# Three transfers of weight words moved to another queue, and ten products moved in front of a join

## The chip, the cores and the metric

The kernel runs on one core of a Trainium2 chip. The metric is the time of one execution on the device, in microseconds (us). Six names occur throughout: TensorE (PE in the profile) multiplies matrices, VectorE (DVE) and ScalarE (ACT) work elementwise, GpSimd (POOL) does the rest, SyncE (SP) only issues transfers, and the DMA engines carry them. ScalarE and GpSimd issue transfers as well, in the order of their own instructions.

## The reference

Two blocks follow one another: a DeltaNet recurrence over 768 tokens for 4 x 8 heads of 48, and a feed-forward block on its output with a layer norm in front and a residual.

```python
# attention: q, k, v of (4, 8, 768, 48), beta of (4, 8, 768)
k_n = k / (np.linalg.norm(k, axis=-1, keepdims=True) + 1e-06)
for t in range(S):
    kt, vt, bt = k_n[:, :, t], v[:, :, t], beta[:, :, t, None]
    y[:, :, t] = np.einsum('bhd,bhde->bhe', q[:, :, t], state)
    v_old = np.einsum('bhde,bhd->bhe', state, kt)
    state = state + bt[:, :, :, None] * np.einsum('bhd,bhe->bhde', kt, vt - v_old)
# bridge: (B, H, S, D) -> x of (4, 768, 384); w_ch1 of 384 x 1536, w_ch2 of 1536 x 384
xn = (x - mu) / np.sqrt(var + 1e-06) * g_ln
out = x + np.maximum(xn @ w_ch1, 0.0) @ w_ch2
```

The weights arrive as 64-bit floats. The kernel gets them as pairs of 32-bit words and makes 32-bit floats of them itself.

## The kernel before

The 768 tokens are cut into twelve chunks of 64. Within a chunk the recurrence becomes a triangular system: the products of the keys (gram, `gsb`) are inverted block by block (VectorE eliminates row after row, names `xb`, `tmp`), and a join puts the inverted blocks of 32 rows together into `xt` with small matmuls (`p_e`, `p_z`). The recurrence of the chunk then needs `xt` (`p_u`), the state (`p_k`, `p_y`, `p_s`), and hands its output, normalised, to the feed-forward block. That block is one chunk behind, so its large products fill TensorE while the recurrence waits.

The weights come in twelve pieces of 768 KB of words, with three buffers for them. A piece is fetched into a buffer and converted in five steps, one on ScalarE and four on VectorE; the next fetch waits until its buffer is free.

```python
    def fetch_words(eng=nc.gpsimd, held=False):
        if len(words) < len(pieces):
            src = pieces[len(words)][1]
            words.append(early_pool.tile([128, WN, 2], U32, name="words", bufs=3))
            if held:
                nc.vector.memset(words[-1][0:1, 0:1, 0].bitcast(FP32), 0.0)
            ...
            eng.dma_start(out=out_, in_=src)
```

With `held`, the first fetch has to wait for a memset of one element, and so for VectorE's place in its program. The start of the kernel, in the order that every engine keeps (`next` runs a generator to its next yield):

```python
        inv = first_blocks(two)                  # blocks of 16 rows of chunks 0 and 1
        for _ in range(3):
            next(inv)                            # gather, roots of the diagonal (ScalarE), scaling
        load_blocks(q, 0, 1, (nc.scalar,))       # eight transfers on ScalarE's queue
        load_kv(0, nc.scalar)                    # four of k, two of v (v_raw), on the same
        for gen in grams_01:
            next(gen, None)                      # ScalarE: four copies of p_g to gsb, line 372
        ...
        for i in range(FB // 2):
            next(inv)                            # VectorE: two rows of the elimination each
            if i == 4:
                for n in range(3):
                    fetch_words(nc.sync, held=(n == 0))
                keep_warm(3, mark=True)          # matmuls on zeros, to keep the clock up
        knrm = norm_parts(0, xts[NXT - 1])
        next(knrm)                               # ScalarE: squares of k, lines 404 and 406
        parts = [to_fp32(i) for i in range(3)]
        joining = first_join(0)
        next(joining)                            # x_n, p_e (line 598), es (ScalarE, line 601)
        turned(0, 1)                             # q turned, VectorE
        knrm = next(knrm)                        # sums (VectorE) and root (ScalarE)
        for piece in parts[0:2]:
            next(piece)                          # first conversion step of words, ScalarE, line 302
        for _ in range(3):
            next(parts[0])                       # lines 304, 306, 310, VectorE
        next(joining)                            # p_z (line 606), own + p_z (line 607)
        ...
        nc.vector.memset(tblocks[3][0:1, 0, 0, 0:1], 0.0)   # line 891: marker for the loads behind it
        load_blocks(q, 1, 1, (nc.sync,))
        load_kv(1)
```

From chunk 2 on a chunk has a slot, written as a list of names in the order of issue; each engine takes its own part of it in that order. The names that matter here: `H` is one product p_h of the hidden layer (six instructions on TensorE) with its relu on ScalarE; `KQ`, `U`, `S`, `PU` are the recurrence's products p_k and p_y, p_u, p_s, and p_y; `P1` to `P7` are the seven half-size products of the second layer (p_a, p_o), `S1` to `S4` and `d1` to `d7` the sums before and after them on VectorE; `R` is all that is left of the rows of an elimination and `r` two rows; `own`, `xt` and `xn` turn and hand over the inverted blocks, `J` is one step of the join, and an apostrophe says that it belongs to the pair of chunks in hand and not to the next; `ga`, `sq`, `no` begin the next pair's inversion (a zeroing on ScalarE and a turning on VectorE; a root on ScalarE; scaling on VectorE). `TQ` and `PT` turn q and multiply it with k, `L1` and `L2` are the layer norm.

The join's three steps on a pair of chunks:

```python
    def join(chunks, both=False):
        ...
        yield                                    # xn: two turnings on VectorE
        for c, xn in zip(chunks, xns):           # J, J
            for h in range(GH):
                for e in range(2):
                    nc.tensor.matmul(p_e[r1, h], gsb[r0, h, BK:C], xn[r0, h])
                if last:
                    last_z(*last, h)             # p_z of the first chunk between the p_e of the second
            if last:
                end_z(*last)                     # half the copy to xt on VectorE, half on ScalarE
            ...                                  # es on ScalarE
            yield
        for h in range(GH):                      # J
            last_z(*last, h)
        end_z(*last)
        yield
```

Of the kernel before, what the change touches and what calls it, by code (L numbers as in the profile page):

```python
# [8 lines left out]
FP32 = mybir.dt.float32  # L9
# [40 lines left out]
@contextmanager  # L50
def in_this_order(tc):

    first = len(tc.nc.cur_bb.bb.instructions)
    last = {}
    yield last
    for ins in tc.nc.cur_bb.bb.instructions[first:]:
        if ins.engine not in ORDERED:
            continue
        if ins.engine in last:
            tc.add_manual_dep(  # L60
                ins, last[ins.engine].name,
                mybir.DependencyInfo(mybir.DependencyClass.NoSync, mybir.DependencyReason.DATA),
                reason="in_this_order",
            )
        last[ins.engine] = ins
# [17 lines left out]
def kernel(  # L83
# [22 lines left out]
    nc = tc.nc  # L106
    B, H, S, D = q.shape
# [41 lines left out]
    def load_blocks(src, c, n, engs):  # L149
        dst = tblocks[(2 * c + n) % NTB]  # L150
        for u in range(2):
            toks = slice(c * C + 32 * u, c * C + 32 * u + 32)
            for hp in range(2):
                for m in range(2):
                    w = min(32, D - 32 * m)
                    p0 = DP * hp + 32 * m
                    engs[m % len(engs)].dma_start(
                        out=dst[p0 : p0 + 32, :, u, 0:w],
                        in_=src[:, hp::2, toks, 32 * m : 32 * m + w].rearrange("b j t d -> t (b j) d"),
                    )  # L160

    def load(dst, src, c, eng):
        for e in range(2):
            eng.dma_start(
                out=dst[e * C : (e + 1) * C],
                in_=src[2 * e : 2 * e + 2, :, c * C : (c + 1) * C, :].rearrange("g h p d -> p (g h) d"),
            )

    def load_k(c, eng):

        for n in range(2):
            for e in range(2):
                eng.dma_start(
                    out=k_of(c)[(e ^ n) * C : (e ^ n) * C + C, n::2],
                    in_=k[2 * e : 2 * e + 2, n::2, c * C : (c + 1) * C, :].rearrange("g h p d -> p (g h) d"),
                )
# [4 lines left out]
    def load_kv(c, eng=nc.sync):  # L181
        load_k(c, eng)
        vs[c] = loads.tile([128, GH, D], FP32, name="v_raw")
        load(vs[c], v, c, eng)
# [23 lines left out]
    ]  # L208
    words = []

    def fetch_words(eng=nc.gpsimd, held=False):
        if len(words) < len(pieces):
            src = pieces[len(words)][1]
            words.append(early_pool.tile([128, WN, 2], U32, name="words", bufs=3))
            if held:
                nc.vector.memset(words[-1][0:1, 0:1, 0].bitcast(FP32), 0.0)
            out_ = words[-1].rearrange("p n w -> p (n w)")
            if len(src.shape) == 3:
                out_ = out_.rearrange("p (t n) -> p t n", t=2)
            eng.dma_start(out=out_, in_=src)  # L220
# [114 lines left out]
    def turned(c, n, more=False):  # L335

        made[c][n] = work.tile([128, GH, C], FP32, name="kq"[n] + "t", bufs=(4, 2)[n])
        nc.vector.transpose(
            made[c][n].rearrange("p i (u t) -> p i u t", t=32), tblocks[(2 * c + n) % NTB]
        )  # L340
        if more and c + 2 < NCH:
            load_blocks((k, q)[n], c + 2, n, (nc.sync,))
# [6 lines left out]
    def gram(c, fine=False, maker=ps_two):  # L349

        kt = made[c][0]
        p_g = ps_g(maker)
        for j in range(GP):
            for u in range(2) if fine else (0,):
                for hp, e in TILES:
                    rows = slice(DP * hp, DP * hp + D)
                    i = e * GP + j
                    r0 = BK * u
                    out_ = p_g[C * e + r0 : C * e + r0 + (BK if fine else C), hp, j, 0 : C - r0]
                    nc.tensor.matmul(  # L360
                        out_, kt[rows, i, r0 : r0 + (BK if fine else C)], kt[rows, i, r0:C]
                    )
        dst = grams[c].rearrange("p (j n) t -> p n j t", n=2)
        if fine:
            nc.scalar.copy(dst[:, :, :, 0:BK], p_g[:, :, :, 0:BK])
            yield
        else:
            nc.scalar.copy(dst, p_g)
        for e in range(2):
            if fine:  # L370
                rows = slice(C * e, C * e + BK)
                nc.scalar.copy(dst[rows, :, :, BK:C], p_g[rows, :, :, BK:C])
            else:
                rows = slice(C * e + BK, C * e + C)
                nc.scalar.copy(dst[rows, :, :, 0:BK], p_g[rows, :, :, BK:C])
# [49 lines left out]
    def new_chunk(c):  # L425
        if c % SLAB == 0:
            pairs[c // SLAB] = work.tile([128, SLAB, GH, C], FP32, name="gsb", bufs=2)
        grams[c] = pairs[c // SLAB][:, c % SLAB]
        made[c] = {}
# [391 lines left out]
    def begin(c):  # L821
        xs[c] = work.tile([128, 2, DM], FP32, name="x_ln")
        xnts[c] = work.tile([128, KC, TOK], FP32, name="xnt")

    def keep_warm(n, width=8, mark=False):

        if mark:
            nc.vector.memset(zeros[0:1, 0:1], 0.0)  # L828
        p_w = ps_ffn([128, 8, 64], "p_w")
        for _ in range(n):  # L830
            nc.tensor.matmul(  # L831
                p_w[0:64, 0:width], zeros, zeros[:, None, :].to_broadcast([128, width, 64]),
                start=True, stop=True,
            )

    two = range(2)
    with in_this_order(tc) as last:
        grams_01 = []
        keep_warm(3)
        for c in two:  # L840
            new_chunk(c)
            turned(c, 0)
            grams_01.append(gram(c, fine=True, maker=(ps_two, ps_by)[c]))
            next(grams_01[c])

        keep_warm(46, 1)
        inv = first_blocks(two)
        for _ in range(3):
            next(inv)
        load_blocks(q, 0, 1, (nc.scalar,))  # L850
        load_kv(0, nc.scalar)
        for gen in grams_01:
            next(gen, None)
        nc.vector.tensor_copy(out=scale_w[:, 0, 0:KC], in_=g_sb)
        nc.vector.tensor_scalar_mul(scale_w[:, 1, 0:KC], g_sb, 2.0**-52)
        for i in range(FB // 2):
            next(inv)
            if i == 4:
                for n in range(3):
                    fetch_words(nc.sync, held=(n == 0))  # L860
                keep_warm(3, mark=True)
        knrm = norm_parts(0, xts[NXT - 1])
        next(knrm)
        parts = [to_fp32(i) for i in range(3)]
        joining = first_join(0)
        next(joining)
        turned(0, 1)
        knrm = next(knrm)
        for piece in parts[0:2]:
            next(piece)  # L870
        for _ in range(3):
            next(parts[0])
        next(joining)
        masking = product(0)
        next(masking)
        to_xt(0)
        joining = join((0,), both=True)
        next(joining)
        next(parts[0], None)
        fetch_words()  # L880
        next(joining)
        next(parts[2])
        scale_v(0, knrm)
        keep_warm(1)
        for _ in joining:
            pass
        for _ in masking:
            pass
        keep_warm(1)

        nc.vector.memset(tblocks[3][0:1, 0, 0, 0:1], 0.0)
        load_blocks(q, 1, 1, (nc.sync,))
        load_kv(1)
        for c in (2, 3):
            load_blocks(k, c, 0, (nc.sync,))
        load_beta()
        begin(0)
        recur_0 = recur(0)
        next(recur_0)
        next(recur_0)  # L900
        keep_warm(1)
        for _ in range(3):
            next(parts[1])
        next(recur_0)
        next(parts[1], None)
        fetch_words()
        next(recur_0)
        keep_warm(4)
        next(recur_0)
        next(parts[2])  # L910
        next(recur_0)
        for _ in parts[2]:
            pass
        fetch_words()
# [42 lines left out]
    with behind(tc, after):  # L957
# [10 lines left out]
        3: """KQ H H sq H no H r H r U TQ(a2) H r H r H r S H r H r H H PU P1 L1 S1 S2 d1 PT(a2)  # L968
            P2 d2 L2 S4 P6 d6 S3 TK(a4) P5 d5 r N r P7 d7 G(a4) TK(b4) P3 d3 r G(b4) Vk P4 d4 r
            Vn Vs""",  # L970
        4: """KQ H H R' own' H H H xt' xn' ga H J' H H sq J' no U H J' r H r S H r TQ(b) H r PU P1
            L1 S1 S2 d1 PT(b) P2 d2 L2 S4 P6 d6 S3 r P5 d5 r N r P7 d7 r P3 d3 r Vk P4 d4 Vn Vs""",
        5: """KQ H r H r H r H r H R U TQ(a2) H H own TK(a4) H S H H xt H xn H PU P1 L1 S1 S2 d1
            PT(a2) P2 d2 L2 S4 P6 d6 S3 TK(b4) J P5 d5 G(a4) N P7 d7 J P3 d3 G(b4) J P4 d4
# [105 lines left out]
```

## Time and profile before

| | |
|---|---|
| time, median of 3 runs | 578.1 us (577.19, 578.1, 581.67) |
| span of the profiled run | 575.6 us |
| mean granted TensorE clock | 0.956 |
| TensorE busy | 533.7 us, 93% |
| VectorE busy | 394.6 us, 69% |
| ScalarE busy | 173.3 us, 30% |
| HBM read | 28.43 MB |

The page cuts the span into 40 slices of 14.4 us and gives the busy share of each in tenths; the row PEclk is the share of the full clock that was granted. A timeline lists the instructions of one engine by start and duration in us; the brackets at the end of a line hold the idle time just before, and what ended it. "ACTq" and "SPq" are issues of transfers from ScalarE and SyncE; their duration is that of the issue and not that of the transfer. Where a wait is for several things at once, the one that came last is named.

### The profile page before, as it was taken

The page shows a single profiled execution, that of the slowest core. Times are in us where ns is not written, and L with a number is a line of the kernel's source. Part 1 is how long each engine was busy: PE and PEld are TensorE (multiplying, and loading weights), DVE is VectorE, ACT ScalarE, POOL GpSimd, SP SyncE. Part 2 cuts the span into 40 slices and gives each one's busy share as a digit, 9 for nine tenths or more (in the row PEclk, how much of TensorE's full clock was granted, in tenths as well). Part 3 has the DMA queues.
Part 4 walks back from the last instruction along what each step waited for, and adds up shares of the span by engine and source line. Part 5 has one row for each costly group of instructions (what it writes and reads, how often), then busy time and mean ns, then how long its engine had stood idle before and what let it go on. Part 6 is the DMA issues. An engine that isn't in the chain of part 4 may idle for free.

```text
span 575.6 us, 20679 instructions
## 1 busy us (share of the span) xinstructions
PE 533.7 (93%) x9386; PEld 459.4 (80%) x9386; DVE 394.6 (69%) x816; ACT 173.3 (30%) x352; POOL 15.4 (3%) x36
## 2 busy tenths in 40 slices
PE   6769797889999996999999999999999999999996
PEld 3445576468898895798888898888898988988996
DVE  4856978999858789499964899736899540523212
ACT  1043352512253242422335322245213232222120
POOL 5000111000000000000000000000000000000000
PEclk9767999999699999899999999999999999999999
DMA  4545968871065144023432304203213010010101
GB/s 58 119 131 114 225 152 212 135 113 30 5 77 97 24 53 87 3 30 70 56 44 60 55 2 84 30 10 77 30 27 59 2 31 1 2 30 1 27 1 27
DMA packets 158390, 34.47 MB, mean 60 GB/s; under 512 B 153680, under 2 KB 156768, under 8 KB 158304
## 3 DMA queue, kind: packets, MB, share of 16 engines
q1 hardware_dynamic: 144208, 24.63, 25.1%
q0 software_dynamic: 1456, 7.10, 3.8%
q10 hardware_dynamic: 12640, 1.44, 1.9%
q8 instruction: 73, 1.20, 0.9%
q14 instruction: 13, 0.11, 0.1%
HBM read 28.43 MB, written 4.72 MB: 58 GB/s over the span
## 4 chain that ended last, share of the span: by engine, by line
PE 65%; DVE 15%; issue 12%; ACT 3%; DMA 3%; POOL 1%; POOLq 0%; DVEq 0%; ACTq 0%
PE p_h L732 26%; PE p_a L787 13%; PE p_o L787 9%; DVE tmp L545 4%; DVE xb L550 4%; PE p_g L360 2%; DMA words<-in_moe_w_ch_dram 2%; PE p_u L651 2%; PE p_y L671 2%; PE p_s L663 2%; PE p_z L614 2%; PE p_g L385 2%; PE p_k L640 1%; PE p_e L570 1%; PE p_y L640 1%
## 5 line engine op out<-in xcount | busy, mean ns | idle before, releaser
L732 PE MATMUL p_h<-xnt,w_sb 128*128 128x256 f32 x864 | 200.6, 389 | 4.3 <-ACT h L736 1.9
L732 PEld LDWEIGHTS p_h<-xnt,w_sb 128*128 128x128 f32 x864 | 163.4, 193 | 29.0 <-issue 2.7
L736 ACT ACTIVATE h<-p_h 128x256 f32<-128x256 f32 x144 | 55.1, 384 | 154.6 <-PE p_h L732 147.8
L550 DVE TENSOR_TENSOR xb<-xb,tmp 128x31 f32<-128x31 f32 (+20 forms) x170 | 56.9, 335 | 5.8
L545 DVE TENSOR_TENSOR tmp<-xb,gb 128x31 f32<-128x31 f32 (+15 forms) x155 | 52.5, 339 | 4.2
L787 PE MATMUL p_o<-w_sb,h 128*128 128x192 f32 x264 | 49.1, 337 | 0.0
L787 PE MATMUL p_a<-t,h 128*128 128x192 f32 x264 | 47.2, 329 | 0.5 <-DVE o L792 0.5
L787 PEld LDWEIGHTS p_o<-w_sb,h 128*128 128x128 f32 x264 | 43.8, 193 | 0.8
L787 PEld LDWEIGHTS p_a<-t,h 128*128 128x128 f32 x264 | 42.7, 190 | 1.2 <-DVE o L792 0.8
L682 DVE BATCH_NORM_STATS2 st<-x_ln 128x6 f32<-128x384 f32 x24 | 13.0, 544 | 36.3 <-ACT x_ln L676 36.2
L831 PE MATMUL p_w<-zeros 128*64 128x64 f32 (+1 forms) x118 | 26.1, 388 | 7.4 <-DVE zeros L828 4.2
L787 PE MATMUL p_a<-t,s 128*128 128x192 f32 x132 | 24.1, 333 | 0.4 <-DVE o L792 0.4
L787 PE MATMUL p_a<-w_sb,h 128*128 128x192 f32 x132 | 24.2, 333 | 0.0
L787 PE MATMUL p_o<-w_sb,s 128*128 128x192 f32 x132 | 23.6, 328 | 0.0
L699 ACT COPY xnt<-p_n 128x384 f32<-128x384 f32 x24 | 10.4, 483 | 43.3 <-PE p_n L698 43.2
L570 PEld LDWEIGHTS p_e<-x_n,gsb 32*32 32x32 f32 x768 | 15.4, 115 | 9.9 <-DVE x_n L561 6.9
L570 PE MATMUL p_e<-x_n,gsb 32*32 32x32 f32 x768 | 17.0, 202 | 6.6 <-DVE x_n L561 6.4
L581 ACT ACTIVATE es<-p_e 32x512 f32<-32x512 f32 x23 | 13.6, 589 | 31.6 <-PE p_e L570 31.3
L787 PEld LDWEIGHTS p_a<-t,s 128*128 128x128 f32 x132 | 22.2, 195 | 0.8 <-DVE o L792 0.7
L831 PEld LDWEIGHTS p_w<-zeros 128*64 128x64 f32 x118 | 10.8, 166 | 14.6 <-issue 6.7
L360 PEld LDWEIGHTS p_g<-kt 48*64 48x64 f32 (+1 forms) x896 | 13.3, 130 | 11.1 <-issue 4.8
L787 PEld LDWEIGHTS p_a<-w_sb,h 128*128 128x128 f32 x132 | 21.3, 190 | 0.6
(124 smaller groups left out, 693.8 us busy)
## 6 DMA issues: line engine op xcount, KB each, us to landing
words<-in_moe_w_ch_dram POOLq DMA_DIRECT2D x9, 768.0 KB, 5.6
out_dram<-o SPq DMA_DIRECT2D x48, 96.0 KB, 2.2
k<-in_k_dram SPq DMA_DIRECT2D x44, 96.0 KB, 3.1
v_raw<-in_v_dram SPq DMA_DIRECT2D x22, 192.0 KB, 3.9
tb<-in_k_dram SPq DMA_DIRECT2D x48, 64.0 KB, 2.5
tb<-in_q_dram SPq DMA_DIRECT2D x44, 64.0 KB, 2.6
words<-in_moe_w_ch_dram SPq DMA_DIRECT2D x3, 768.0 KB, 6.5
tb<-in_q_dram SPq DMA_DIRECT2D x44, 32.0 KB, 2.6
```

The source lines that it names most:

```text
L360: nc.tensor.matmul(out_, kt[rows, i, r0 : r0 + (BK if fine else C)], kt[rows, i, r0:C])
L385: nc.tensor.matmul(p_g[half(e ^ hp), hp, j], kt[rows, i], qt[rows, i])
L545: nc.vector.tensor_tensor(out=t, in0=xb[:, :, 0:n, j : j + 1].to_broadcast([128, nb, n, w]), in1=gb[:, :, j : j + 1, j + 1 : L].to_broadca ...
L550: nc.vector.tensor_tensor(out=rest, in0=rest, in1=t, op=ALU.subtract)
L570: nc.tensor.matmul(p_e[r1, h], gsb[r0, h, BK:C], xn[r0, h])
L581: nc.scalar.mul(es[r1], p_e[r1], -1.0)
L614: nc.tensor.matmul(p_z[r0, h], es[r1, h], xt[r1, h, BK:C])
L682: nc.vector.bn_stats(out=st[:, g], in_=y[:, g])
L732: nc.tensor.matmul(p_h, w1_sb[:, t, f * 128 : (f + 1) * 128], xnt[:, t], start=(t == 0), stop=(t == KC - 1),)
L736: nc.scalar.activation(h[f // HF][:, f % HF], p_h, ACTF.Relu)
L787: nc.tensor.matmul(p[n], a[:, f], b[:, f], start=(first and f == 0), stop=(f == HF - 1), skip_group_check=True,)
L831: nc.tensor.matmul(p_w[0:64, 0:width], zeros, zeros[:, None, :].to_broadcast([128, width, 64]), start=True, stop=True,)
```

## The change

It has two parts. The three first fetches of words are no longer issued by SyncE behind the fifth step of the elimination; ScalarE issues them, right behind the values of chunk 0. The memset that held them back is gone. In the slot of chunk 4, the fifth one, four h products that stood in or behind the join now stand in front of it, and the names around the join are put in a new order to match: `ga` moves behind the join's first step, and the rows `r` close up where products between them are gone. The first part is for the order of the transfers in the start, the second for TensorE's work while VectorE finishes the elimination.

```diff
-    def fetch_words(eng=nc.gpsimd, held=False):
+    def fetch_words(eng=nc.gpsimd):
         if len(words) < len(pieces):
             src = pieces[len(words)][1]
             words.append(early_pool.tile([128, WN, 2], U32, name="words", bufs=3))
-            if held:
-                nc.vector.memset(words[-1][0:1, 0:1, 0].bitcast(FP32), 0.0)
...
         load_blocks(q, 0, 1, (nc.scalar,))
         load_kv(0, nc.scalar)
+        for _ in range(3):
+            fetch_words(nc.scalar)
         for gen in grams_01:
             next(gen, None)
...
             next(inv)
             if i == 4:
-                for n in range(3):
-                    fetch_words(nc.sync, held=(n == 0))
                 keep_warm(3, mark=True)
...
-        4: """KQ H H H R' own' H H H xt' xn' ga H J' H H sq J' no U H J' r H r S H r TQ(b) H r PU P1
+        4: """KQ H H H H H R' own' H H H xt' xn' H H J' ga H sq J' no U H J' r r S r TQ(b) r PU P1
             L1 S1 S2 d1 PT(b) P2 d2 L2 S4 P6 d6 S3 r P5 d5 r N r P7 d7 r P3 d3 r Vk P4 d4 Vn Vs""",
```

## The prediction

> **What bounds the kernel now.** I read the page first, then the chain of waits, then the timeline of the two places that the change touches, and the waits there. The page says that TensorE is busy 93% of the span and that from the eighth slice on its row stands at 8 or 9 almost throughout. The chain of waits gives TensorE 65% of the span and VectorE 15%. So time is to be won only where TensorE stands or runs at half clock; the change touches two such places.
>
> ```profile
> PE   6769797889999996999999999999999999999996
> PEclk9767999999699999899999999999999999999999
> ```
>
> The first place is the start. The timeline of ScalarE (start, duration, queue or engine, line, operation, count, and in brackets its idle time):
>
> ```profile
> 16.36 4.99 ACTq L157 DMA_DIRECT2D tb<-in_q_dram  x8
> 21.38 2.83 ACTq L173 DMA_DIRECT2D k<-in_k_dram  x4
> 29.34 1.33 ACTq L164 DMA_DIRECT2D v_raw<-in_v_dram  x2
> 30.71 2.34 ACT L372 COPY gsb<-p_g 32x512 f32<-32x512 f32 x4 [14.11 <-DMA words<-in_moe_w_ch_dram]
> 33.08 0.52 ACT L404 ACTIVATE xt<-k 128x384 f32<-128x384 f32 x1
> 33.63 1.07 ACT L406 ACTIVATE xt<-k 64x384 f32<-64x384 f32 x2
> 34.72 0.38 ACT L601 ACTIVATE es<-p_e 128x256 f32<-128x256 f32 x1
> ```
>
> The reader is to see the hole between 24.2 (21.38 + 2.83) and 29.34. ScalarE has issued q and k and stands before the first issue of the values, although nothing has ever used that tile. What ends its wait is a transfer of words. The records of the two issues in the trace say why: v's first issue waits on semaphore 117, and the DMA before it that counts up 117 is the first transfer of words, issued by SyncE at 24.47. Its sixteenth count arrives at 29.32, and v goes out at 29.34. The DMAs of SyncE and ScalarE take their completion semaphores from one set of eight (numbers 100, 102 to 105, 115 to 117), each waiting until the last user of its semaphore has landed. So v waits for data that it has nothing to do with. Behind v, in ScalarE's order, stand the four copies of gsb, the squares of k, and es, for which TensorE waits:
>
> ```profile
> 29.83 1.44 PE L598 MATMUL p_e<-x_n,gsb 32*32 32x16 f32 x128
> 35.25 1.79 PE L606 MATMUL p_z<-own,es 32*32 32x16 f32 x118 [3.98 <-ACT es L601]
> ```
>
> p_e is done at 31.27; its es starts at 34.72, which is 3.45 later.
>
> The second place is the fifth slot (c=4), the only one after 110 us in which TensorE waits for more than 1.6 us at a time. TensorE's timeline there, then VectorE's, then the busy time of a stretch (length; busy of PE, PE loads, VectorE, ScalarE, GpSimd; clock, DMA share, GB/s):
>
> ```profile
> 215.79 8.04 PE L732 MATMUL p_h<-xnt,w_sb 128*128 128x256 f32 x36
> 228.91 1.92 PE L570 MATMUL p_e<-x_n,gsb 32*32 32x32 f32 x64 [5.08 <-DVE x_n L561]
> 230.76 4.72 PE L732 MATMUL p_h<-xnt,w_sb 128*128 128x256 f32 x12
> ...
> 262.66 2.22 PE L787 MATMUL p_a<-t,h 128*128 128x192 f32 x12 [0.53 <-DVE o L792]
> ```
>
> ```profile
> 236.74 0.68 DVE L619 COPY xt<-p_z 32x512 f32<-32x512 f32 x1 [5.49 <-PE p_z L614]
> ...
> 241.89 0.68 DVE L619 COPY xt<-p_z 32x512 f32<-32x512 f32 x1 [2.18 <-PE p_z L614]
> ```
>
> ```profile
> 246.00:256.00 10.00, 10.00 (x174) 9.24 (x173) 9.69 (x22) 1.81 (x4) 0.00 (x0) 1.00 0.32 41
> ```
>
> Six h products (36 instructions, 1.30 us each product) end at 223.8; then TensorE stands 5.08 us until VectorE has eliminated, turned and handed over x_n at 228.87. The next twelve h instructions take 4.72 instead of 2.6: the clock is at one half from 227.7 to 234.6. From 241.89 on VectorE has no gap; at 262.66 TensorE waits for it. So after the join VectorE sets the end of the slot, and what counts is when its copy at 241.89 can start.
>
> [...] Here that issue time is 0.35 to 0.43 us for each of the three transfers, and the change puts it on ScalarE. [...] The clock records agree: their stretches are multiples of 3.413 us, and the one at 227.7 follows a window with no matmul at all.
>
> **Part 1, the words.** Removed: the one-element memset on VectorE (0.06) and SyncE's three issues. Added: three issues on ScalarE behind v, 3 x 0.43 = 1.3. Now step by step. v can go at 24.2, since the semaphores ahead of it are now those of q, landed by 23.8; it takes 1.33, the words 1.3, so the copies of gsb start at 26.8 instead of 30.71. I add 0.4 for a fuller queue: 27.2. Copies 2.34, to 29.6; squares 1.6, to 31.2 (k has landed at 27.7 even today). p_e does not move: it starts at 29.83, when the warming matmuls end and x_n is there, and ends at 31.27. So es starts at about 31.4 instead of 34.72: 3.3 less. After es come the norm of k and the first conversion of words (35.43 today, about 32.1 then). For it the words must be there. v is 2.3 us of transfer (32.2 to 34.5 today) and would end near 28.5; the words follow in the same queue at today's pace (6.4 us for the three), so the first lands near 31 and the third near 35. Today they land at 29.3, 31.2 and 33.6. The first is just in time; the third is needed at 43.8 today, 40 then. VectorE's three conversion steps and the addition to own (39.01 today) then come 3.3 to 3.5 earlier. Everything up to the first h products hangs on this chain, the later fetches of words and the loads behind the marker of line 891 too, so I let the stretch to 212 us shift as a whole: **minus 3.4**.
>
> **Part 2, the fifth slot.** Nothing is added: twelve products before and after. Before the join stand ten instead of six, 10 x 1.30 = 13.0 from 215.79, to 228.8. x_n is there at 228.87, so the idle 5.08 is filled to within 0.1 and costs no delay. From x_n to VectorE's copy of the second chunk, today 228.87 to 241.89:
> - p_e of the first chunk at full clock, about 1.13 as at 293.5, instead of 1.92: minus 0.8
> - one h product at 1.30 instead of two at half clock, 4.65: minus 3.35
> - the second p_e with p_z (1.24), the two copies (1.36), p_u (1.14), one h product (1.49), the last p_z (1.15): unchanged.
>
> The sum is minus 4.15: the copy starts at 237.7. VectorE's work behind it is the same, and in the same order (two steps of rows, s_all, rows, the turning of q, rows, then statistics). TensorE has no h products left between p_s and P1: it would reach P1 some 7 us earlier, and then waits some 3 us for VectorE in PT, P6, P7 and P4. The end moves by VectorE's 4.15. The zeroing of xb and the gather (ga) behind the first join step cost nothing: ScalarE is free then, and VectorE does the gather in the same place.
>
> From this I take off an expected 0.8. Between 231 and 236 the new order has small matmuls, 1.3 idle, and one h product. Much fuller windows of small matmuls with some idle time were followed by half clock elsewhere (after 67 to 70.7, and after 94.6 to 98). One such window costs about 1.7, and I give it one chance in two. **Minus 3.3.**
>
> Sum: 578.1 - 3.4 - 3.3 = 571.4. Today's runs lie at 577.2, 578.1 and 581.7, so a typical one is slightly below the median; I say **571.0**.
>
> **Rivals.** First: the words behind k and v run into a full queue, and ScalarE stands in the issue itself. For it: the eighth issue of q took 1.39 instead of 0.50, and an issue of v on SyncE at 57.9, with words under way, took 3.49. Against it: words are only 128 pieces each, and nothing else is under way at 25. A stall of 2 us would leave 1.5 of part 1: 573. Second: half clock after the join, as above; with two windows of it the slot gives only 1 to 2: 573. Third: the start's gain is absorbed by the transfers, which are busy 79 to 99% from 50 to 80. For it: the chain of waits runs through words up to 100. Against it: these transfers are released by the work that moves forward, and they do not queue up from an earlier time. Absorbed wholly: 574.5. Fourth, upward: with ScalarE no longer late, TensorE's gap of 3.98 before p_z shrinks to 0.5, and the clock, at one half from 33.2 to 50.2, might stay up; small products there run twice as long as later, and up to 3 us would come on top: 568. I doubt it, since 32x32 products alone did not raise the clock in that stretch.
>
> **Range and chances.** Both parts whole, with the fourth: 567.5; one of them lost: 574 to 575. I take 567.5 to 575. Faster by 2% means below 566.5, more than the two parts and the fourth give: 0.04. Slower by 2% would need a stall that nothing here shows: 0.02. Within 2%: 0.94.
>
> **What would show it.** In the changed profile v must go out near 24.2 and not near 29.3, followed by three issues of about 0.43; gsb near 27, es near 31.4, and the addition to own near 35.6. In the fifth slot 60 h instructions must run without a gap up to x_n, p_e in about 1.1, and the second copy of xt must follow x_n by about 8.9 instead of 13.0. I am wrong if the issues of words take over 1 us each, if the words land after ScalarE asks for them, if the difference at 200 us is much less than 3.4, or if TensorE runs at half clock between the join and P1.

## The result, and the profile after

The changed kernel takes 572.1 us (median of 4 runs, 569.9 to 573.0); the kernel before, beside it, 578.8 (577.19 to 581.67). The ratio is 0.987, with a 95% interval from 0.982 to 0.992. The profiled span falls from 575.6 to 570.5 us. (In the removed line of the printed diff one `H` too many stands in front of `R'`: the slot before begins `KQ H H R' own' H H H xt' xn' ga H J'`, six products ahead of the join, as the prediction counts.)

The page's two rows first, TensorE's busy tenths and its granted clock:

```profile
PE   6579896989899999889999999999999999999996
PEclk9758998999699999899999999999999999999999
```

The start and the slot are too fine for these rows. ScalarE's timeline of the start, in the changed kernel:

```profile
15.41 4.87 ACTq L157 DMA_DIRECT2D tb<-in_q_dram  x8
20.32 2.74 ACTq L173 DMA_DIRECT2D k<-in_k_dram  x4
23.09 1.37 ACTq L164 DMA_DIRECT2D v_raw<-in_v_dram  x2
24.50 1.75 ACTq L218 DMA_DIRECT2D words<-in_moe_w_ch_dram  x3
26.30 2.34 ACT L370 COPY gsb<-p_g 32x512 f32<-32x512 f32 x4 [10.63 <-DMA v_raw<-in_v_dram]
28.66 0.52 ACT L402 ACTIVATE xt<-k 128x384 f32<-128x384 f32 x1
29.21 1.07 ACT L404 ACTIVATE xt<-k 64x384 f32<-64x384 f32 x2
30.30 0.38 ACT L599 ACTIVATE es<-p_e 128x256 f32<-128x256 f32 x1
```

The hole ahead of v is gone. v goes out directly behind k, its two issues now wait on the semaphores of q (105 and 115, whose q transfers landed at 20.72 and 20.89), and es starts 0.16 us after p_e ends at 30.14. What TensorE and VectorE make of it:

```profile
28.89 1.25 PE L596 MATMUL p_e<-x_n,gsb 32*32 32x16 f32 x128 [0.79 <-DVE x_n L591]
30.83 1.79 PE L604 MATMUL p_z<-own,es 32*32 32x16 f32 x118 [0.69 <-ACT es L599]
35.06 0.34 PE L604 MATMUL p_z<-own,es 32*32 32x16 f32 x10 [2.44 <-issue]
```

```profile
33.12 1.02 DVE L308 SCALAR_TENSOR_TENSOR words<-words,scale_w 128x768 f32<-128x768 uint32 x1
35.44 0.42 DVE L605 TENSOR_TENSOR own<-own,p_z 128x256 f32<-128x256 f32 x1 [1.30 <-PE p_z L604]
```

p_z no longer waits 3.98 us for es, but ten matmuls before its end TensorE stands 2.44 us, and "issue" means that the profile shows nothing it waits for. VectorE is free at 34.14 and waits 1.30 for those ten. Before, the same hole was there, shorter, at the same matmul, and VectorE waited 0.45 behind it:

```profile
38.62 0.34 PE L606 MATMUL p_z<-own,es 32*32 32x16 f32 x10 [1.58 <-issue]
```

```profile
39.01 0.42 DVE L607 TENSOR_TENSOR own<-own,p_z 128x256 f32<-128x256 f32 x1 [0.45 <-PE p_z L606]
```

TensorE's timeline of the fifth slot, then two lines of VectorE's, then the stretch behind the join (length; busy of PE, PE loads, VectorE, ScalarE, GpSimd; clock, DMA share, GB/s):

```profile
212.75 13.22 PE L730 MATMUL p_h<-xnt,w_sb 128*128 128x256 f32 x60
225.96 1.20 PE L568 MATMUL p_e<-x_n,gsb 32*32 32x32 f32 x64
...
231.59 1.70 PE L649 MATMUL p_u<-v_raw,xt 64*64 64x48 f32 x62 [0.30 <-ACT xt L617]
233.22 2.60 PE L730 MATMUL p_h<-xnt,w_sb 128*128 128x256 f32 x6
...
243.11 1.16 PE L383 MATMUL p_g<-qt,kt 48*64 48x64 f32 x64 [2.01 <-DVE qt L336]
...
257.74 2.22 PE L785 MATMUL p_a<-t,h 128*128 128x192 f32 x12 [1.16 <-DVE o L790]
```

```profile
230.24 0.68 DVE L617 COPY xt<-p_z 32x512 f32<-32x512 f32 x1 [1.94 <-PE p_z L612]
...
236.99 0.68 DVE L617 COPY xt<-p_z 32x512 f32<-32x512 f32 x1 [3.77 <-PE p_z L612]
```

```profile
231.00:236.00 5.00, 4.70 (x86) 3.79 (x88) 2.08 (x6) 2.66 (x5) 0.00 (x0) 0.66 0.01 3
```

Sixty h instructions run without a gap up to x_n. Behind the join the clock is 0.66 of full over these five us: the records have one window of 3.4 us at one half, from 231.9, and p_u and the h product in it are slow.

Where the 5.1 us of span came from, by marks in both traces (first issue of q; own + p_z; first h of the fifth slot; first h of the slot behind it; end):

| stretch | before | after | difference |
|---|---|---|---|
| start to first issue of q (not touched) | 16.36 | 15.41 | -0.95 |
| to own + p_z | 22.65 | 20.03 | -2.62 |
| to the fifth slot | 176.78 | 177.31 | +0.53 |
| the fifth slot | 51.03 | 49.15 | -1.88 |
| to the end | 308.76 | 308.58 | -0.18 |

The first row belongs to no part of the change: in the profiled runs of this study the first issue of q lies anywhere between 14.9 and 16.6. Times below are therefore counted from that issue.

### The profile page after: what moved, and what is told of

The parts are those of the page before. It is cut to its first block, busy times and chain, and to the rows that moved or that the text cites. A ratio compares the mean times of both kernels' runs of the same rounds, so it can differ in the third digit from the quotient of the medians.

```text
span 570.5 us, 20678 instructions
## 1 busy us (share of the span) xinstructions
PE 530.6 (93%) x9386; PEld 458.2 (80%) x9386; DVE 394.4 (69%) x815; ACT 173.3 (30%) x352; POOL 15.5 (3%) x36
## 4 chain that ended last, share of the span: by engine, by line
PE 72%; SPq 9%; DVE 7%; ACT 4%; issue 3%; DMA 2%; ACTq 1%; DVEq 0%
PE p_h L730 31%; PE p_a L785 13%; PE p_o L785 10%; SPq L157 6%; PE p_u L649 2%; PE p_z L612 2%; PE p_k L638 2%; PE p_g L358 2%; PE p_g L383 2%; PE p_e L568 2%; PE p_y L669 2%; PE p_s L661 2%; PE p_y L638 2%; DVE tmp L543 1%; DVE xb L548 1%
## 5 line engine op out<-in xcount | busy, mean ns | idle before, releaser
L785 PE MATMUL p_o<-w_sb,h 128*128 128x192 f32 x264 | 47.9, 331 | 0.0
L829 PE MATMUL p_w<-zeros 128*64 128x64 f32 (+1 forms) x118 | 23.6, 357 | 8.5 <-DVE zeros L826 5.3
L785 PE MATMUL p_a<-w_sb,h 128*128 128x192 f32 x132 | 24.2, 333 | 0.0
L358 PE MATMUL p_g<-kt 48*64 48x64 f32 (+2 forms) x896 | 15.5, 225 | 7.5 <-DVE s_all L664 3.0
L829 PEld LDWEIGHTS p_w<-zeros 128*64 128x64 f32 x118 | 9.6, 149 | 15.7 <-issue 6.8
L579 ACT ACTIVATE es<-p_e 32x512 f32<-32x512 f32 x23 | 13.6, 589 | 27.9 <-PE p_e L568 27.6
L785 PEld LDWEIGHTS p_o<-w_sb,s 128*128 128x128 f32 x132 | 21.6, 190 | 0.1
```

The lines of the kernel that those rows point to most:

```text
L358: nc.tensor.matmul(out_, kt[rows, i, r0 : r0 + (BK if fine else C)], kt[rows, i, r0:C])
L579: nc.scalar.mul(es[r1], p_e[r1], -1.0)
L785: nc.tensor.matmul(p[n], a[:, f], b[:, f], start=(first and f == 0), stop=(f == HF - 1), skip_group_check=True,)
L829: nc.tensor.matmul(p_w[0:64, 0:width], zeros, zeros[:, None, :].to_broadcast([128, width, 64]), start=True, stop=True,)
```

## The experiments

All medians stand beside runs of the kernel before on the same chip: 578.24 in the first group (a0 and e1 to e3), 578.26 in the second (e4, e5, e6, e8), 578.95 in the third. The edits are against the changed kernel.

### Each part alone, and both again

e1 keeps the words' part and has the old slot:

```diff
-        4: """KQ H H H H H R' own' H H H xt' xn' H H J' ga H sq J' no U H J' r r S r TQ(b) r PU P1
+        4: """KQ H H R' own' H H H xt' xn' ga H J' H H sq J' no U H J' r H r S H r TQ(b) H r PU P1
```

> Part 1 alone: the three words fetches behind v on ScalarE, the fifth slot as before. Theory (v waited on a semaphore shared with the words): v goes out near 24.2 after the start of its own queue (directly behind k), the addition to own comes about 2.6 us earlier once the two starts are laid over each other at the first q issue (16.36 before, 15.41 in the changed kernel), the fifth slot keeps its idle of about 5 us and its half clock; time about 575.3, ratio 0.995. Rival (the start's gain is absorbed by the transfers before 212 us): time within 0.5 of before, though own is earlier.

e2 keeps the slot's part and has the old start (with `held` and its memset in `fetch_words`, not printed here):

```diff
-        for _ in range(3):
-            fetch_words(nc.scalar)
...
             if i == 4:
+                for n in range(3):
+                    fetch_words(nc.sync, held=(n == 0))
```

> Part 2 alone: the new order of the fifth slot, the start as before. Theory: from the slot's first h product to the copy of the second chunk 24.2 us instead of 26.1 if one window at half clock falls behind the join, 22.0 if none does; time 574.0 to 576.3, ratio 0.993 to 0.996. Rival (the order itself is slower at the join, for instance the second p_e with p_z at 1.6): about 24.2 with the clock at full. In either case VectorE is without a gap from that copy to the last product of the slot.

> The changed kernel again, beside its parts: the sum of what the two parts give alone, within 1 us, if they do not touch each other; about 572.

| | median (runs) | ratio to before, 95% | own after q | fifth slot |
|---|---|---|---|---|
| before | 578.24 (55) | | 22.65 | 51.03 |
| e1, words only | 575.65 (22) | 0.996 (0.994 to 0.998) | 20.58 | 51.20 |
| e2, slot only | 573.29 (12) | 0.992 (0.989 to 0.996) | 22.65 | 47.26 |
| a0, both | 574.03 (12) | 0.991 (0.987 to 0.994) | 20.52 | 49.14 |

Each part moves only its own stretch. By the ratios they are worth 2.4 and 4.4 us, and both together 5.4: the intervals, some 1.3 to 1.9 us to either side, do not say whether 1.4 is lost in between. The expectation of a0, the sum of the parts within 1 us and about 572, is not met by the point values (574.03), nor refuted; e2 took less than the 574.0 to 576.3 expected. The slot says where some of it can go. e2 fell on no window at half clock behind the join; a0 fell on the same one as the first run of the changed kernel. The two lines of e2 that answer to those above:

```profile
232.17 1.14 PE L651 MATMUL p_u<-v_raw,xt 64*64 64x48 f32 x62 [0.30 <-ACT xt L619]
233.24 1.56 PE L732 MATMUL p_h<-xnt,w_sb 128*128 128x256 f32 x6
```

1.14 and 1.56 instead of 1.70 and 2.60: 1.6 of the 1.88 us by which the slot is shorter in e2 (47.26 against 49.14). What follows VectorE's second copy of xt up to the next slot takes 24.93 us before, 24.91 after, 24.90 in e2 and 24.94 in e1: nothing behind that copy has changed, and it sets the end of the slot.

### Is it the shared semaphore, or ScalarE's queue?

In e3 the words stay behind the fifth elimination step, with their memset, but GpSimd issues them instead of SyncE; the slot is the old one. In the trace of the kernel before, GpSimd's fourteen transfers count on the semaphores 107 to 114, and the 323 of SyncE and ScalarE on the eight that the prediction lists; these three count on 112 to 114.

```diff
             if i == 4:
                 for n in range(3):
-                    fetch_words(nc.sync, held=(n == 0))
+                    fetch_words(nc.gpsimd, held=(n == 0))
```

(this diff is against the kernel before.)

> The kernel before with one word changed: the first three words fetches, at the same place and behind the same memset, are issued by GpSimd, whose semaphores are another set. Theory (the shared semaphore): v goes out directly behind k although the words go out at the same time as before; gsb follows v at once, es starts within 0.2 of the end of p_e, and the time is that of part 1 alone within 1 us. Rival (v was held by the words' traffic on the DMA engines, or by ScalarE's own queue being full): v still goes out some 5 us behind k, and the time is that of before.

The words go out from 23.54, at the place that they had; ScalarE's timeline:

```profile
23.02 1.37 ACTq L164 DMA_DIRECT2D v_raw<-in_v_dram  x2
24.43 2.34 ACT L372 COPY gsb<-p_g 32x512 f32<-32x512 f32 x4 [9.02 <-DMA k<-in_k_dram]
...
29.95 0.38 ACT L601 ACTIVATE es<-p_e 128x256 f32<-128x256 f32 x1 [1.53 <-PE p_e L598]
```

v follows k at once, although words are still issued at the same time: its first issue goes out 0.5 ahead of the first words, its second, at 23.71, behind them. So the hole was the semaphore that v shared with words, and ScalarE's queue as such has no merit. That an issue waits for the last user of its semaphore the kernel before shows throughout: of 236 transfers of SyncE and ScalarE for which the trace has that user's landing, none is issued ahead of it. Why it has to wait is not shown. es now waits for p_e and no longer for ScalarE. The time is 576.33 (22 runs), 0.997 (0.995 to 0.999): no better than e1, though ScalarE is saved the issues. TensorE's hole in p_z is the longest of all here, and own comes 20.99 after q, later than in e1 (20.58):

```profile
30.48 1.17 PE L606 MATMUL p_z<-own,es 32*32 32x16 f32 x118 [0.59 <-ACT es L601]
35.76 0.34 PE L606 MATMUL p_z<-own,es 32*32 32x16 f32 x10 [4.12 <-issue]
```

### The window at half clock behind the join

Two ways to fill TensorE there: e4 leaves nine products in front of the join and puts the tenth between the join's second step and p_u; e5 keeps the ten and adds two matmuls on zeros (`W`) before p_u.

```diff
-        4: """KQ H H H H H R' own' H H H xt' xn' H H J' ga H sq J' no U H J' r r S r TQ(b) r PU P1
+        4: """KQ H H H H H R' own' H H H xt' xn' H J' H ga sq J' H no U H J' r r S r TQ(b) r PU P1
```

```diff
-... xn' H H J' ga H sq J' no U H J' ...
+... xn' H H J' ga H sq J' W no U H J' ...
```

> The changed kernel with one h product taken from in front of the join and put into the hole between the join's second step and p_u (nine in front instead of ten, one after each of the three join steps that follow). Theory (the slot lost half of its gain to one window at half clock, which the hole and the small matmuls bring on): with the hole filled the clock stays at full behind the join; from the slot's first h product to the second copy 22.3 us instead of 24.2, to the next slot's first h product 47.2 instead of 49.1; time 1 to 2 us under the changed kernel where that had the half window. Rival (the loss is in the order of the join's steps, clock or no clock): 24.2 stays.

> The changed kernel with one more instruction group: a matmul on zeros (512 columns, two instructions, about 1.0 us at full clock) in the same hole. It adds work and moves no product. Theory (clock): no window at half clock between the join and P1, 22.4 us to the second copy. Rival (the zeros count too little for the clock, or delay p_u): 24.2 or more.

> The changed kernel with nine h products instead of ten ahead of the join in the fifth slot, as in e4_nine_front, taken again beside its own variants. If nine is really better than ten: a median of 570 to 572 us and no window at half clock between the join and the next slot's first h. If the earlier result was a lucky phase of the half-clock windows: 572 to 574 us, with such a window in the profile.

| | median (runs) | ratio to before, 95% | fifth slot | half clock between join and second copy |
|---|---|---|---|---|
| e4 | 571.34 (6) | 0.990 (0.987 to 0.993) | 47.38 | none |
| e4 again | 573.54 (14) | 0.992 (0.989 to 0.995) | 47.89 | none |
| e5 | 573.83 (6) | 0.993 (0.989 to 0.996) | 47.62 | none |

In the slot both do what they were made for: 47.4 to 47.9 instead of 49.15. None of the five profiled kernels with nine products and this join (e4, e4 again, and e7, e9, e10 below) has half clock there; of the four with ten and no filling, three have (the changed kernel twice, and e6 below) and one has not (e2). Without the window the order with ten is as short (e2, 47.26). In the time it does not show; e4 again, 573.54 without a window, fits neither of the two outcomes that were named for it: 571.3 and 573.5 for the same program stand against 572.1 and 574.0 for the changed one. The window's cost in one run is 1.9 us; how often it falls there, these few profiles do not say.

e8 takes e4 and moves the turning of q on VectorE forward, since TensorE waits for it (2.01 us in the changed kernel, at 243.11 above; 1.45 in e4 again).

```diff
-... sq J' H no U H J' r r S r TQ(b) r PU P1
+... sq J' H no TQ(b) U H J' r r S r r PU P1
```

> As e4, and the turning of q (1.24 us of VectorE) is moved from behind the join's last copy to VectorE's idle stretch in front of it. Theory (from the last copy on VectorE without a gap sets the end of the slot): the slot ends 1.24 earlier than in e4, 46.0 us from its first h product to the next slot's. Rival (TensorE or the copy itself has become the bound): 47.2 as in e4.

TensorE's timeline in e8:

```profile
241.26 1.41 PE L383 MATMUL p_g<-qt,kt 48*64 48x64 f32 x64
242.60 2.22 PE L785 MATMUL p_o<-w_sb,h 128*128 128x192 f32 x12
246.80 3.90 PE L785 MATMUL p_a<-t,s 128*128 128x192 f32 x12 [1.98 <-DVE o L790]
...
257.52 2.22 PE L785 MATMUL p_a<-t,h 128*128 128x192 f32 x12 [0.31 <-DVE o L790]
```

The wait for q is gone, but part of it turns up again one sum later, 1.98 at 246.80, and a window at half clock behind it makes 3.90 of 2.22. In sum TensorE's waits for VectorE behind the second copy fall from 4.04 (e4 again) to 2.29; the window takes back 1.68, and VectorE stands 0.75 for the slow p_a. The slot takes 47.74, as in e4, not the 46.0 expected; the median is 572.48 (6 runs), 0.991 (0.989 to 0.994). Whether the 1.24 would come out with the clock at full stays open.

### TensorE's hole in p_z

The idle time inside p_z has nothing that releases it. The trace has a DMA queue "q8 instruction", with 73 packets of 16,384 bytes (1.20 MB) in the kernel before and in the changed one. One of them is under way at 32.53 to 33.55 in the changed kernel, where the 118th matmul ends and the hole begins, and one at 36.19 to 37.29 in the kernel before. So I read the hole as TensorE's wait for its own instructions; the traces name no releaser. TensorE's trace of the kernel before has 18,854 instructions: each matmul is two, a load of weights and the product (9386 of each), and 82 are others. Behind 14 us it has three places where a small matmul without a wait of its own starts 0.7 us or more behind the one before: in p_z at 38.62 (1.79), in another p_z at 69.46 (1.21) and in p_g at 82.19 (1.14). They lie 1280 and 512 instructions apart, 5 and 2 times 256, and 73 times 256 is 18,688, nearly all that TensorE has. By this count p_z with 128 matmuls is one whole block of 256. e6 takes 40 of the 46 warming products at the start away (and makes the other 6 wider), e9 seven; each is two matmuls in the trace, four instructions.

```diff
-        keep_warm(46, 1)
+        keep_warm(6)       # e6
+        keep_warm(39, 1)   # e9, with the slot of e4
```

> The changed kernel with the first warming group cut to 12 wide matmuls instead of 92 narrow ones, of about the same time (6.7 us), so that 160 instructions fewer stand in front of p_z on TensorE. Theory (the gap of 2.3 to 2.65 us inside p_z, ten matmuls before its end, is a wait for instructions): the gap leaves that place and turns up 80 matmuls later, in the products behind p_z or the next p_e; own then follows VectorE's third conversion step, about 1.2 us earlier. Rival (p_z waits there for data): the gap stays at the 118th matmul of p_z.

> As e4_again with 28 instructions fewer in the warming matmuls ahead of p_e, so that the border of the 256-instruction blocks falls some matmuls behind the end of p_z instead of ten before it. Theory: p_z runs without a hole, own + p_z starts when VectorE is free (about 1.3 us earlier than in e4_again after the first q issue), and the hole turns up in the masking product behind it, so the join's p_e gains less than 1.3 us, 0 to 0.7. Rival (the hole follows the place in the stage, not the count of instructions): it stays ten matmuls before the end of p_z and nothing moves.

TensorE in e6, for the places and not for the times, then in e9:

```profile
31.65 0.77 PE L604 MATMUL p_z<-own,es 32*32 32x16 f32 x70 [0.59 <-ACT es L599]
35.55 0.98 PE L604 MATMUL p_z<-own,es 32*32 32x16 f32 x58 [3.13 <-issue]
```

```profile
30.99 0.24 PE L604 MATMUL p_z<-own,es 32*32 32x16 f32 x4 [0.58 <-ACT es L599]
34.83 1.89 PE L604 MATMUL p_z<-own,es 32*32 32x16 f32 x124 [3.60 <-issue]
36.65 0.48 PE L383 MATMUL p_g<-qt,kt 48*64 48x64 f32 x4
38.71 1.97 PE L383 MATMUL p_g<-qt,kt 48*64 48x64 f32 x60 [1.58 <-issue]
```

The hole follows the count of instructions. With 28 fewer it moves by 14 matmuls, from the 118th to the 132nd, which is the fourth of p_g; and a block of 256 earlier another border comes in, at the fourth of p_z. With 160 fewer it moves by 80, less the 128 of a block: 118 + 80 - 128 = 70; at the border behind that, in p_e, stands only a gap of 0.24 (38.98). So the block is 256 instructions in these traces. The same count, with one more for each separate semaphore instruction in TensorE's trace, holds through the whole kernel: of the fourteen profiles, all 54 places where a matmul without a wait of its own starts 0.7 us or more behind the one before lie on such a border, the three of the kernel before and three of the changed one among them (after 14 us, warming matmuls and slow products of 384 columns left out). They are not confined to the start: the changed kernel has one of 1.64 us in p_z at 145.87, e2 one of 1.65 in p_y at 154.60, e9 one of 1.60 in p_y at 240.81. So an edit that moves the borders moves every later hole too, and the medians of e6, e9 and e10 carry all of them. My expectation for e9, that p_z would be free of it, was wrong in arithmetic: a product of one whole block holds a border wherever one shifts it, unless it begins on one. e9 pays twice, with own 21.04 after q, only 0.11 earlier than in e4 again, and takes 574.71 (22 runs), 0.992 (0.990 to 0.994). e6's 573.44 (20 runs), 0.992 (0.990 to 0.995), is no gain over the changed kernel either.

e10 adds to e9 that the masking product goes from in front of the join's p_e to behind it, and that a warming product is left out. (That product stood behind p_e, not ahead of it as the expectation says; the masking product takes its place.)

```diff
         next(joining)
-        masking = product(0)
-        next(masking)
         to_xt(0)
         joining = join((0,), both=True)
         next(joining)
         next(parts[0], None)
         fetch_words()
         next(joining)
+        masking = product(0)
+        next(masking)
         next(parts[2])
         scale_v(0, knrm)
-        keep_warm(1)
```

> As e9_hole_out_of_pz, and the masking product goes behind the first join's p_e, without the single warming matmul ahead of p_e. Theory: with the hole out of the path and nothing ahead of p_e but x_n, the join's p_e starts about 1.3 us earlier than in e4_again after the first q issue, and the time falls by 0.8 to 1.3 us, to about 570. Rival (TensorE falls back to half clock, or the hole moves into p_e itself): p_e is reached earlier by less than 0.5 us or lasts longer by as much, and the time stays within 0.5 us.

The second hole is off the path: its packet lands at 37.48, while p_e still waits for x_n, and p_e starts 22.88 after q instead of 24.90 in e9. But that is what e4 again has (22.98), as p_z still has its hole, now of 3.59. 574.89 (9 runs), 0.991 (0.988 to 0.995): nothing gained.

What makes the hole longer than before? e7 takes e4 and issues the third piece's words only after ScalarE's first conversion steps, so that fewer words are under way.

```diff
-        for _ in range(3):
+        for _ in range(2):
             fetch_words(nc.scalar)
...
         for piece in parts[0:2]:
             next(piece)
+        fetch_words(nc.scalar)
```

> As e4_again, but ScalarE issues the third piece's words only behind its first conversion steps of the first two pieces, not directly behind v. Theory (TensorE's wait for its instructions inside p_z grows because the packet meets the words' transfers): the hole inside p_z falls from 2.3 to 3.7 us to 1.6 to 1.8, own + p_z starts about 0.8 us earlier after the first q issue (19.3 us instead of about 20.1), and the time falls by 0.5 to 1 us against e4_again. Rival (the hole's length has nothing to do with the words): it stays at 2.3 us or more and the time stays within 0.5 us. Second rival: the later words hold up the third piece, and the h products of the first slot start later.

TensorE in e7, then VectorE:

```profile
31.37 1.32 PE L604 MATMUL p_z<-own,es 32*32 32x16 f32 x118 [0.73 <-ACT es L599]
34.47 0.34 PE L604 MATMUL p_z<-own,es 32*32 32x16 f32 x10 [1.78 <-issue]
...
40.21 0.53 PE L568 MATMUL p_e<-x_n,gsb 32*32 32x32 f32 x11 [1.17 <-issue]
```

```profile
34.66 1.02 DVE L308 SCALAR_TENSOR_TENSOR words<-words,scale_w 128x768 f32<-128x768 uint32 x1
35.60 0.41 DVE L605 TENSOR_TENSOR own<-own,p_z 128x256 f32<-128x256 f32 x1
```

Start to start the hole is 1.99 here, against 3.15 and 3.75 in e4. From the start of p_z to the first matmul behind the hole TensorE takes 3.10 us, the shortest of all; before it takes 3.37 and e2 3.39, both with the words landed by then; the runs with all three words under way take 3.8 to 5.3. The packet itself takes 0.9 to 1.3 us in all (1.10 before, 1.02 in the changed kernel), and the first matmul follows 1.2 to 1.5 us behind its end (1.33 and 1.51); what differs is when it starts, 0.6 us behind the start of p_z in e7, 0.9 in before and e2, 1.4 to 2.6 in the others (1.70 in the changed kernel). That speaks for the transfers as what delays the packet; how they do it no run shows, and each figure is from one profile. own comes 19.67 after q, the earliest of all, now with VectorE and not TensorE last, as ScalarE waited 0.91 for the first words. But the next hole, 256 instructions on, then lies inside the join's p_e (1.17 at 40.21), and the last p_e matmul starts 24.58 after q, as in e4 again (24.69). The first h product comes at 41.08 after q against 40.97. So the start is no shorter at its end. The median, 571.01 (6 runs), 0.987 (0.983 to 0.992), is the lowest of the last group but overlaps e4 again's interval and equals the changed kernel's ratio; I do not call it faster.

## Why the prediction was right, and where it was not

**The wait of v: right.** "v can go at 24.2": it went out at 23.09, directly behind k as there (7.68 after q; 24.2 is 7.84 after q). "the words 1.3", plus 0.4 for a fuller queue: 1.75. gsb near 27: 26.30; es near 31.4: 30.30, each about a microsecond early since q was. es comes 3.47 earlier counted from q, against 3.3 (2.67 in a0 and 2.88 in e1, where the issues of q and of the words took longer). The words were there when ScalarE asked for them, but for 0.65 us at the second piece in e1. e3 shows that the cause named, the shared semaphore, is the cause. The first rival, an issue that stalls, was there at 0.4 to 0.6 us only (1.75 to 1.93 for the three instead of 1.3, nearly all of it in the first: 0.79, in a0 and e1 0.94 and 0.97).

**"VectorE's three conversion steps and the addition to own come 3.3 to 3.5 earlier": mis-sized.** The conversion steps came 3.46 earlier after q (2.66 in a0, 2.87 in e1), but own only 2.62 (2.13 in a0, 2.07 in e1). That own started at 35.44, with 35.6 named, is luck: q had begun 0.95 earlier. The missing term is TensorE's hole inside p_z, which I had not seen in the kernel before although it stood there, 1.58 of idle time: it grew by 0.5 to 0.9, and VectorE then waited for p_z.

**"I let the stretch to 212 us shift as a whole: minus 3.4": too much.** The fifth slot began 2.09 earlier after q (1.90 in a0, 1.25 in e1). The part between own and the slot took 0.5 longer than before, with 32.7 us at half clock instead of 28.3. Single profiles don't settle why: this part takes 175.7 to 180.4 us in all of them but e6's. In e2 and e3, whose program is the old one there, it took 175.80 with 23.7 us at half clock and 177.49 with 27.9, before 176.78 with 28.3; so the windows explain the spread in part at most. The third rival, the whole gain absorbed by the transfers, would have left e1 within 0.5 us of before, and e1 gained 2.4; that a part of it is absorbed stays open.

**The ten products: right.** "the idle 5.08 is filled to within 0.1": p_e started 13.21 after the first h, 13.12 before. From p_e to the second copy I had 8.8 without half clock; e2 took 9.16, of which 0.19 is the h product, 1.49 from start to start and not 1.30. So minus 4.15 was minus 3.74 (slot stretch to the copy, 26.10 to 22.36). "The end moves by VectorE's 4.15": the next slot starts 24.9 us behind the copy in every one of these kernels but e8 (24.73), so the end does move with the copy. TensorE's waits for VectorE behind it came too, 4.6 us in sum (2.01, 1.43 and 1.16) and not some 3.

**The window at half clock: right in kind and size.** "One such window costs about 1.7, and I give it one chance in two." It came in the profile, and in its repeat, but not in e2, and cost 1.88. Why it falls there in one run and not in another is not shown. The clock records of the kernel before and the changed one have stretches that are multiples of 3.413 us, but for the last, and the stretches fall differently in two runs of one program: the first 118 matmuls of the start's p_z take 1.79 us in e4 and 1.17 in e4 again. The fourth rival, a clock that would stay up in the start, did not come: 17.1 us at half clock from 30.5, as before from 33.2.

**The sum.** Predicted -3.4 and -3.3. In the profiled pair the parts gave -2.1 up to the slot and -1.9 in it, 4.0 in all; the other 1.1 of the span came from the untouched start and end. That 571.0 lay so near 572.1 is luck in part: in a0, with twelve runs, the changed kernel gained 5.4 us by its ratio (0.991), 1.3 less than the 6.7 of the sum, and took 574.0. By the ratios of e1 and e2 the words gave less than was said (2.4 for 3.4) and the slot more (4.4 for 3.3), though both intervals hold what was said. And two of the signs named for being wrong did appear: the difference ahead of the slot was much less than 3.4, and TensorE ran at half clock between the join and P1. The range held for both medians of the changed kernel, 572.1 and 574.0, and "within 2%" was not in doubt.

## What to carry to other kernels

When an engine stands before the issue of a transfer whose buffer was never used, look up which semaphore that issue waits on and who counted it up last; moving the other transfer freed the issue both ways here (behind v on ScalarE, and on GpSimd), where it had stood 5.1 us. When a wait on a chain is removed, look for the next one in the same product, an "issue" gap too: of 5.1 us at the issue 2.7 to 3.5 reached es, 2.1 to 2.6 own, and 2.4 the time. Products put in front of a join filled TensorE's idle 5.08 us there, but behind the join three of the four profiles of that order have half clock, at a cost of 1.88 us in the first; so judge them with the clock behind the join, and over many runs.

## What I had not expected of the hardware

- TensorE's holes lie on a count of 256 of its own instructions (1280 and 512 apart in the kernel before), so a product of 128 small matmuls, 256 instructions, holds such a place unless it begins on one; in the p_z of the start it is 1.8 to 3.8 us from one matmul to the next there (4.3 in e3). Of the large products, the h products of the kernel before pass such places at 407.3, 434.4 and 550.9 with their usual 0.22; but at 305.5 in e2 it is 1.16.
- The same program differs by some ten us from run to run (the kernel before from 573.4 to 584.6 in one group of 55), and single profiles of one program differ in which stretches fall on half clock. With 22 runs the interval was 1.3 us to either side (e1), with six 1.4 to 2.6 (e4, e5, e7, e8), so a gain of 2 us needs some twenty runs to be seen.
- One window at half clock costs about 1.9 us where TensorE is the bound (the join) and next to nothing where VectorE is: e9 and e10 had one from 242.3 and 240.9, and the next slot started 24.90 and 24.89 us behind their second copy, as in e4 again (24.90).
